# Value products summed by accumulating DMAs, and the ends of a scan and its corrections by VectorE

## The chip, the cores and the metric

The kernel runs on one core of a Trainium2 chip. The metric is device time in microseconds (us) of one execution; the median of several runs is compared. The core has TensorE (matmuls, into the PSUM memory), VectorE and ScalarE (elementwise work), GpSimd and SyncE, and sixteen DMA engines that the queues of SyncE, ScalarE and GpSimd feed. Each engine takes its instructions strictly in its written order, and an instruction that waits holds up all that stand behind it on its engine.

## What is computed

Two independent parts share the core, and their outputs are concatenated. Part A is a state space layer, part B a local, dilated attention:

```python
# A: x (1, 2048, 448), 448 complex states
Lam_bar = exp(dt * Lam);  B_bar = ((Lam_bar - 1) / Lam)[:, None] * Bmat
h[t] = Lam_bar * h[t-1] + B_bar @ x[t]
y = 2 * (h @ Cmat.T).real + x * Dskip
# B: 16 heads of 28, each token sees itself and 7 tokens at distances 2, 4 .. 14
attn = softmax(q . k[pos - 2*w] / sqrt(28) over w = 0..7, masked where pos - 2*w < 0)
o = sum over w of attn[w] * v[pos - 2*w];  out_b = o @ wo
```

## The kernel before

Part B holds 16 consecutive tokens in each of 128 partitions. Queries, keys and values come from TensorE, the logits from products on VectorE that TensorE sums, and the softmax weights `attn` are made for two halves of eight tokens. The value sums (`pv`, L437 and L440) are the longest work of VectorE: for each half two blocks of four tokens, so four blocks in all, in the order half 1 tokens 0 to 3, half 1 tokens 4 to 7, half 0 tokens 0 to 3, half 0 tokens 4 to 7. A block makes eight products `attn[w] * vd` of 128x1792 elements (L437), one for each w, and adds seven of them to the first (L440). The very last product and addition are cut into two halves. The tile `pvb` holds seven such arrays: three accumulators in turn and four products in turn. When a block is summed, `tail` transposes it by DMA on SyncE's queue into `oT` (L453), and TensorE multiplies it by `wo` (L462, `wo_ps`); the results are copied and stored.

Part A is a scan. With four tokens to a step, the level-1 sums of seven tiles m of 128 states (64 states, real and imaginary) are kept as `h[0]` to `h[3]`, each 128x512. A log-step scan (`scan`, L699 to L709) works on groups of sixteen tokens, for the tiles in three parts `MH` (0 to 3, 4 and 5, 6). Then:

- `ends` (L711) makes, for each m, the state at the end of every four tokens, `G[:, m]`. Seven matmuls go into one PSUM tile `gt` (L723): an identity matmul of 384 columns that brings in `h[3]`, five matmuls with powers of the transition, and an identity matmul of 128 columns that brings in the scan's result. ScalarE copies `gt` to `G` (L725).
- `correct` (L728) adds to `h[b][m]` (b from 0 to 2) what came in from earlier tokens, `mats[b + 1] @ G` (L733, PSUM tile `co`). Where VectorE does it, it adds `co` to `h` in place (L737) and `co` comes from the PSUM tag "pt" with two buffers. Where ScalarE does it (two of the 21), TensorE also adds `h` by an identity matmul (L732), ScalarE copies the sum back (L735), and the tag is "mm" with four buffers.
- `y` (L744) makes the output for 128 groups r and one of the four tokens b: four matmuls with the skip diagonal (L749) and seven with C (L753), a copy to `ya` (L756) and a store on SyncE's queue (L757).

The order of work in the last third is written out by hand. `vchain` chains VectorE's instructions, `chain` TensorE's. TensorE's list `line` holds the two corrections by ScalarE, the `wo` matmuls of the second block, sixteen `y` in the order b = 3, 0, 1, 2 (r from 0 to 3), the `wo` matmuls of the third block after (1, 3), and those of the fourth at the end. On VectorE, `each` is called for every operation of blocks three and four and, from the tenth on, puts one correction behind it. The matching `co` matmuls are spread over `line` by a count of estimated times:

```python
    for ins, dt in line:
        if n < len(extra) and t >= 1.55 * n:
            cx.chain(extra[n][0])
            t, n = t + extra[n][1], n + 1
```

GpSimd sets constants, gives small memsets that order matmuls (L139), and clears parts of `pbuf` and `G` in `alloc_scan`.

Of the kernel before, what the change touches and what calls it, by code (L numbers as in the profile page):

```python
# [12 lines left out]
ALU = mybir.AluOpType  # L13
AX = mybir.AxisListType
f32 = mybir.dt.float32
# [5 lines left out]
NCH = 128  # L21
# [15 lines left out]
PL = 64  # L37
NST = 7
PAD = 64
MH = ((0, 4), (4, 6), (6, 7))  # L40
# [3 lines left out]
KPOW = [1, 2, 3, 4, 8, 12] + [T << s_ for s_ in range(NST)]  # L44
NPW = len(KPOW)
BEGIN = [0, 20, 39]
WEAVE = [38, 55, 73, 85, 101, 112, 129, 140]


class Ctx:  # L50
# [41 lines left out]
    def vchain(self, ins):  # L92
        if self.vtail is not None:
            self.order(ins, self.vtail, "NoSync")
        self.vtail = ins

    def lanes(self, groups, weave=()):

# [62 lines left out]
class PartB:  # L161
# [94 lines left out]
    kdone, product = [0] * 8, None  # L256
# [166 lines left out]
    def pv(self, hf, at, jl0, jl1, last=False, between=(), each=lambda ins: None):  # L423
# [18 lines left out]
            yield between[w - 1](ins) if 0 < w <= len(between) else []  # L442
        self.outs.append(self.tail(hf, jl0, acc, last))

    def tail(self, hf, jl0, acc, last):
        nc, pool, cx = self.nc, self.pool, self.cx
        if self.oT is None:
            self.oT = pool.tile([KA, 2, 14, NCH], bf16, name="oT", tag="bX")
        oT, flat = self.oT[:, self.oi % 2], acc.rearrange("p j d h -> p (j d h)")
        self.oi += 1  # L450
        n = 7 if last else 14
        for c in range(0, 14, n):
            nc.sync.dma_start_transpose(oT[:, c:c + n], flat[:, c * KA:(c + n) * KA])  # L453

        def out(i):
            done = []
            for odd in range(2):
                n = D // 2 if last and i and odd else D
                for c, eng, q in ((0, "A", nc.sync), (n, "V", nc.scalar))[:D // n]:
                    ps = cx.ps([NCH, n], f32, "wo_ps", "lg" if n == D else "mm")  # L460
                    for k in range(KT):
                        done.append(nc.tensor.matmul(ps[:], lhsT=oT[:, 7 * i + 3 * odd + k, :], rhs=self.wo_p[:, odd, k, c:c + n],  # L462
                                                     start=(k == 0), stop=(k == KT - 1)).ins)
                    yb = cx.ya[:, 4 + 2 * i + odd] if last and n == D else pool.tile([NCH, n], bf16, name="yb", tag="yb", bufs=4)[:]
                    cx.ev(eng, yb, ps[:])
                    q.dma_start(self.out_b[:, hf * HJ + jl0 + 2 * i + odd, c:c + n], yb)
            return done

        return out if last else lambda: [out(i) for i in range(2)]


class PartA:
# [84 lines left out]
    def params(self, after):  # L557

        nc, pool, V, pt, kv = self.nc, self.pool, self.nc.vector, self.pt, self.kv
        ident = self.cx.ident  # L560

        def sm(name, shape):
            return pool.tile([NCH] + shape, f32, name=name)

        def wide(v):
# [27 lines left out]
        w, w4, ri = sm("w", [2, NM]), sm("w4", [2, 2, NM]), sm("ri", [2, NM])  # L593
# [13 lines left out]
        self.mats = {}  # L607

    def skip(self):
        nc, ident = self.nc, self.cx.ident  # L610
# [32 lines left out]
                  pool.tile([NCH, NM, 4 * NCH], bf16, name="h3", tag="pr", bufs=2)]  # L643

    def alloc_scan(self):
        pool = self.pool
        self.pbuf = [[pool.tile([NCH, m1 - m0, PAD + NCH], bf16, name=f"pbuf{m0}{i}", tag=f"pbuf{m0}{i}" if m0 else ("lgs", "e")[i]) for i in range(2)]
                     for m0, m1 in MH]
        for pb in self.pbuf:
            for t_ in pb:  # L650
                self.cx.order(self.nc.gpsimd.memset(t_[:, :, 0:PAD], 0.0).ins, self.cx.relay, "NoSync")
        self.G = pool.tile([NCH, NM, 2 + NF], bf16, name="G", tag="q0")
        self.cx.order(self.nc.gpsimd.memset(self.G[:, :, 0:1], 0.0).ins, self.cx.relay, "NoSync")

    def level1(self, mh):
        nc, cx = self.nc, self.cx
# [52 lines left out]
            nc.scalar.copy(dst[:, :, PAD:], ps[:])  # L709

    def ends(self, mh):  # L711
        nc, cx = self.nc, self.cx
        M, v = self.mats, self.h[3]
        hc = self.pbuf[mh][NST % 2]
        for m in range(*MH[mh]):
            vm = v[:, m, :]
            hp = hc[:, m - MH[mh][0], PAD - 1:PAD - 1 + NCH]
            ps = cx.ps([NCH, NF], f32, "gt", "mm")
            mm = [(cx.ident[:], vm[:, 0:3 * NCH], 0, 3), (M[4][:, m, :], vm[:, 0:2 * NCH], 1, 3),
                  (M[8][:, m, :], vm[:, 0:NCH], 2, 3), (M[4][:, m, :], hp, 0, 1), (M[8][:, m, :], hp, 1, 2),  # L720
                  (M[12][:, m, :], hp, 2, 3), (cx.ident[:], hc[:, m - MH[mh][0], PAD:PAD + NCH], 3, 4)]
            for i, (l_, r_, c0, c1) in enumerate(mm):
                nc.tensor.matmul(ps[:, c0 * NCH:c1 * NCH], lhsT=l_, rhs=r_, start=(i == 0), stop=(i == 6),  # L723
                                 skip_group_check=True)
# [231 lines left out]
```

## Time and profile before

| | |
|---|---|
| time, median of 3 runs | 140.66 us (140.31 to 140.9) |
| time of the profiled execution | 141.59 us |
| span of its instructions | 140.0 us |
| TensorE (PE) busy | 133.4 us, 95% |
| VectorE (DVE) busy | 125.0 us, 89% |
| ScalarE (ACT) busy | 86.3 us, 62% |
| GpSimd (POOL) busy | 10.2 us, 7% |
| mean TensorE clock granted | 0.995 of full speed |
| L437, products | 33, 34.5 us busy |
| L440, additions | 29, 30.5 us busy |
| L737, corrections by VectorE | 19, 13.0 us busy |

The profile is of one execution, and its span runs from the first to the last instruction; the remainder of its time lies around the span. The length given for a VectorE or TensorE instruction overlaps with the next one's, so a pace is read from start to start. A wait on a semaphore is named by the engine whose signal came last.

### The profile page before, as it was taken

To read this page: it belongs to the slowest core of one execution; us is meant where nothing else is said; L and a number is where in the kernel's file an instruction comes from. 1 tells how busy PE (TensorE), PEld (TensorE's weight loads), DVE (VectorE), ACT (ScalarE), POOL (GpSimd) and SP (SyncE) were. 2 spreads that over 40 slices of the span, in tenths; PEclk is the share of its full clock that TensorE was granted. 3 is DMA by queue.
4 is the path that set the end of the run, shared out by engine and by line. 5 is a ranking of instruction groups with operands and counts; after the bars stand their busy time and mean duration, and the time that the engine had idled before them with its cause. 6 is when DMAs were issued, how large, how long until landed. Compare 5 with 4: busy or idle time off the path is not lost.

```text
span 140.0 us, 3262 instructions
## 1 busy us (share of the span) xinstructions
PE 133.4 (95%) x1241; PEld 77.7 (56%) x1245; DVE 125.0 (89%) x159; ACT 86.3 (62%) x192; POOL 10.2 (7%) x104
## 2 busy tenths in 40 slices
PE   6999999999999999999999999999999999999970
PEld 2566544544676645455566655678555555555540
DVE  4589999989999999999999999999999999999010
ACT  2677678776785663695599868899633333344360
POOL 7301110001111001100120000000000000000000
PEclk9999999999999999999999999999999999999998
DMA  3999999999954979990024000532125521122842
GB/s 91 317 173 232 175 213 179 150 128 177 202 111 83 180 115 249 248 247 0 0 50 81 5 0 0 103 95 68 37 98 123 140 70 66 66 98 98 197 136 66
DMA packets 44798, 17.03 MB, mean 122 GB/s; under 512 B 37539, under 2 KB 44401, under 8 KB 44783
## 3 DMA queue, kind: packets, MB, share of 16 engines
q1 hardware_dynamic: 44309, 16.30, 56.4%
q10 hardware_dynamic: 474, 0.52, 1.1%
q8 instruction: 10, 0.16, 0.5%
q14 instruction: 5, 0.04, 0.1%
HBM read 3.91 MB, written 3.67 MB: 54 GB/s over the span
## 4 chain that ended last, share of the span: by engine, by line
PE 83%; ACT 10%; DVE 2%; issue 1%; POOL 0%; ACTq 0%; DVEq 0%
PE y_ps L753 15%; PE qk_ps L130 14%; PE v_ps L130 9%; PE l1h L130 8%; PE l L661 7%; PE wo_ps L462 6%; PE lg L346 6%; PE co L733 3%; PE gt L723 2%; PE warm L73 2%; PE y_ps L749 2%; PE l L706 2%; ACT pbuf L709 2%; ACT h L674 2%; ACT h L672 1%
## 5 line engine op out<-in xcount | busy, mean ns | idle before, releaser
L437 DVE TENSOR_TENSOR pvb<-attn,vd 128x1792 bf16<-128x1792 bf16 (+1 forms) x33 | 34.5, 1055 | 0.0
L440 DVE TENSOR_TENSOR pvb<-pvb 128x1792 bf16<-128x1792 bf16 (+1 forms) x29 | 30.5, 1051 | 0.2
L130 PE MATMUL qk_ps<-xbT,wqkv_nat 64*128 64x512 bf16 (+1 forms) x168 | 21.4, 351 | 0.1
L756 ACT CAST ya<-y_ps 128x448 bf16<-128x448 f32 x16 | 8.5, 532 | 18.9 <-PE y_ps L753 18.9
L335 DVE TENSOR_TENSOR pr<-q,kd 128x3072 bf16<-128x3072 bf16 x11 | 19.0, 1751 | 0.4 <-ACT q L156 0.4
L753 PE MATMUL y_ps<-Ccat,h 128*128 128x448 bf16 x84 | 19.0, 353 | 0.0
L130 PE MATMUL l1h<-xaT,Bcat 64*128 64x512 bf16 x112 | 15.7, 377 | 0.0
L462 PE MATMUL wo_ps<-wo_p,oT 128*128 128x448 bf16 (+1 forms) x68 | 14.3, 341 | 0.1
L130 PEld LDWEIGHTS <-wqkv_nat 64*128 64x128 bf16 x168 | 9.1, 94 | 8.5 <-POOL spot L139 1.9
L156 ACT CAST kd<-qk_ps 128x512 bf16<-128x512 f32 (+4 forms) x26 | 10.4, 426 | 5.0 <-PE qk_ps L130 4.4
L130 PE MATMUL v_ps<-wqkv_nat,xbT 64*128 64x448 bf16 x112 | 13.1, 360 | 0.0
L737 DVE TENSOR_TENSOR h<-co,h 128x512 bf16<-128x512 f32 x19 | 13.0, 686 | 0.0
L661 PE MATMUL l<-xaT,Bcat 128*128 128x512 bf16 x45 | 12.6, 379 | 0.1
L156 ACT CAST q<-qk_ps 128x512 bf16<-128x512 f32 (+2 forms) x23 | 9.9, 460 | 1.4 <-PE qk_ps L130 1.3
L753 PEld LDWEIGHTS <-h 128*128 128x128 bf16 x84 | 7.5, 98 | 5.6
L130 PEld LDWEIGHTS <-xbT 64*128 64x128 bf16 x112 | 7.4, 144 | 4.1 <-issue 1.4
L709 ACT CAST pbuf<-l 128x512 bf16<-128x512 f32 (+2 forms) x21 | 8.9, 426 | 1.0 <-PE l L706 0.8
L139 POOL MEMSET spot<- 1x1 f32 x59 | 5.2, 88 | 58.2 <-PE qk_ps L130 25.4
L156 ACT CAST vd<-v_ps 128x448 bf16<-128x448 f32 x16 | 7.6, 534 | 2.9 <-PE v_ps L130 2.8
L130 PEld LDWEIGHTS <-Bcat 64*128 64x128 bf16 x112 | 6.4, 94 | 5.2 <-issue 0.8
L462 PEld LDWEIGHTS <-oT 128*128 128x128 bf16 x68 | 6.4, 97 | 5.0 <-issue 0.2
L335 DVE TENSOR_TENSOR kd<-q,kd 128x3072 bf16<-128x3072 bf16 x5 | 8.8, 1753 | 0.5 <-ACT q L156 0.4
(135 smaller groups left out, 214.1 us busy)
## 6 DMA issues: line engine op xcount, KB each, us to landing
out_dram<-ya SPq DMA_DIRECT2D x19, 112.0 KB, 1.7
out_dram<-yb SPq DMA_DIRECT2D x12, 112.0 KB, 1.7
vd<-vd SPq DMA_DIRECT2D x1, 784.0 KB, 5.7
vd<-vd SPq DMA_DIRECT2D x1, 588.0 KB
xn<-in_B_x_dram SPq DMA_DIRECT2D x2, 224.0 KB, 2.7
wqkv_nat<-in_B_wqkv_dram ACTq DMA_DIRECT2D x2, 224.0 KB, 4.8
wqkv_nat<-in_B_wqkv_dram SPq DMA_DIRECT2D x2, 224.0 KB, 4.3
cn<-in_A_C_re_dram SPq DMA_DIRECT2D x4, 98.0 KB, 3.5
```

The source lines that it names most:

```text
L130: ins = mm(g["ps"], lhsT=l_, rhs=r_, start=first, stop=not (g["left"][0] or g["left"][1]), skip_group_check=True).ins
L156: return self.nc.scalar.copy(out, in_).ins
L335: self.queued(V.tensor_tensor(pr, q[0][:, qu].unsqueeze(2).to_broadcast([KA, KT - 1, 4, n]), self.shifted(self.kT[:, 2 * i + qu], s), op=A ...
L346: out.append(mm(lg[32 * t:32 * t + 32, n * qu:n * qu + n], lhsT=l_, rhs=r_, start=not (s or qu or c), stop=(s == 1 and c == KT - 1), skip_ ...
L437: each(V.tensor_tensor(t_[:, c0:c1], at[:, w, jl0 + c0:jl0 + c1, :].unsqueeze(2).to_broadcast([NCH, c1 - c0, DH, H]), self.vd[:, off + c0: ...
L440: ins = V.tensor_tensor(acc[:, c0:c1], acc[:, c0:c1], t_[:, c0:c1], op=ALU.add).ins
L462: done.append(nc.tensor.matmul(ps[:], lhsT=oT[:, 7 * i + 3 * odd + k, :], rhs=self.wo_p[:, odd, k, c:c + n], start=(k == 0), stop=(k == KT ...
L661: nc.tensor.matmul(ps[:], lhsT=self.Bcat[:, m, k, :], rhs=self.xT[:, b, k, :], start=(k == 0), stop=(b == 0 and k == KT - 1))
L709: nc.scalar.copy(dst[:, :, PAD:], ps[:])
L737: cx.vchain(nc.vector.tensor_tensor(h, ps[:], h, op=ALU.add).ins)
L753: out.append(nc.tensor.matmul(ps[:], lhsT=self.state(m, r, b), rhs=self.C[:, m, :], start=False, stop=(m == NM - 1), skip_group_check=True ...
L756: nc.scalar.copy(ya, ps[:])
```

## The change

- A new function `pv_paired` takes the place of `pv` for the second, third and fourth blocks. It makes the products of w = 0 to 5 in pairs; behind each pair GpSimd's queue issues a DMA that adds the pair's second product to its first, in SBUF (`accum_op=ALU.add`, 128x1792 elements): three DMAs to a block, nine in all. The products of w = 6 and 7 are added by VectorE, and then the three sums of the pairs: four additions to a block in place of seven. The product of w = 7 is written where the second product of the first pair was, and the accumulator is always `pvb[:, 0]`. In the fourth block only the last addition is cut in two; its products are whole.
- `ends` leaves out both identity matmuls. ScalarE copies the scan's result to the fourth token's places of `G`, once for each of the three parts, and for each m a new `join` on VectorE adds `gt` (now 384 columns) and `h[3]` into the other three. `JOINS` places one join behind operation 7 of blocks three and four, and six behind operation 9.
- All 21 corrections are VectorE's. From the tenth operation on, each is followed by two corrections in place of one, and the `co` matmuls stand at every 1.0 of the estimated time in place of 1.55.
- `gchain` keeps GpSimd's order: the memsets of `alloc_scan`, then the DMAs.

```diff
+JOINS = {7: 1, 9: 6}
...
+    def pv_paired(self, hf, at, jl0, each, last=False):
+        nc, V, n, b = self.nc, self.nc.vector, 4, self.pvb
...
+        for w in range(0, 6, 2):
+            t_, u_ = b[:, 1 + w], b[:, 2 + w]
+            product(w, t_)
+            product(w + 1, u_)
+            self.cx.gchain(nc.gpsimd.dma_start(t_.rearrange("p j d h -> p (j d h)"), u_.rearrange("p j d h -> p (j d h)"),
+                                               accum_op=ALU.add).ins)
+        acc, u_ = b[:, 0], b[:, 2]
+        product(6, acc)
+        product(7, u_)
+        add(acc, u_)
+        add(acc, b[:, 1])
+        add(acc, b[:, 3])
+        for c0, c1 in ((0, 2), (2, 4)) if last else ((0, 4),):
+            add(acc, b[:, 5], c0, c1)
+        self.outs.append(self.tail(hf, jl0, acc, last))
...
     def ends(self, mh):
-        hc = self.pbuf[mh][NST % 2]
-        for m in range(*MH[mh]):
+        hc, m0, m1 = self.pbuf[mh][NST % 2], *MH[mh]
+        Gv = self.G[:, :, 1:1 + NF].rearrange("p m (c a) -> p m a c", a=4)
+        nc.scalar.copy(Gv[:, m0:m1, 3], hc[:, :, PAD:PAD + NCH])
+        for m in range(m0, m1):
...
-            mm = [(cx.ident[:], vm[:, 0:3 * NCH], 0, 3), (M[4][:, m, :], vm[:, 0:2 * NCH], 1, 3),
-                  (M[8][:, m, :], vm[:, 0:NCH], 2, 3), (M[4][:, m, :], hp, 0, 1), (M[8][:, m, :], hp, 1, 2),
-                  (M[12][:, m, :], hp, 2, 3), (cx.ident[:], hc[:, m - MH[mh][0], PAD:PAD + NCH], 3, 4)]
+            mm = [(M[4][:, m, :], vm[:, 0:2 * NCH], 1, 3), (M[8][:, m, :], vm[:, 0:NCH], 2, 3), (M[4][:, m, :], hp, 0, 1),
+                  (M[8][:, m, :], hp, 1, 2), (M[12][:, m, :], hp, 2, 3)]
...
-            nc.scalar.copy(self.G[:, m, 1:1 + NF].rearrange("p (c a) -> p c a", a=4),
-                           ps[:].rearrange("p (a c) -> p c a", a=4))
+            self.joins.append((m, ps))
+
+    def join(self):
+        m, ps = self.joins.popleft()
+        self.cx.vchain(self.nc.vector.tensor_tensor(
+            self.G[:, m, 1:1 + NF].rearrange("p (c a) -> p a c", a=4)[:, 0:3], ps[:].rearrange("p (a c) -> p a c", a=3),
+            self.h[3][:, m, 0:3 * NCH].rearrange("p (a c) -> p a c", a=3), op=ALU.add).ins)
...
-    deque(b.pv(1, soft[1][1], 4, 8), 0)
     a.alloc_scan()
+    b.pv_paired(1, soft[1][1], 4, cx.vchain)
...
-    todo = [(b_, m) for b_ in range(3) for m in range(NM)][2:]
+    todo = [(b_, m) for b_ in range(3) for m in range(NM)]
...
-        if len(steps) >= 10 and todo:
-            extra.extend(a.correct(*todo.pop(0), "V"))
+        for n in range(JOINS.get(len(steps), 0)):
+            a.join()
+        if len(steps) >= 10:
+            for n in range(2):
+                if todo:
+                    extra.extend(a.correct(*todo.pop(0), "V"))
...
-    for m in range(2):
-        line += a.correct(0, m, "A")
     line += wo_line(wo[1]())
-    deque(b.pv(0, at0, 0, 4, each=each), 0)
-    deque(b.pv(0, at0, 4, 8, True, each=each), 0)
+    b.pv_paired(0, at0, 0, each)
+    b.pv_paired(0, at0, 4, each, True)
...
-        if n < len(extra) and t >= 1.55 * n:
+        if n < len(extra) and t >= n:
```

More of the change, by code (lines that the diff above doesn't have):

```diff
@@ L95, in vchain, with gchain @@
         self.vtail = ins
+    gtail = None
+    def gchain(self, ins):
+        if self.gtail is not None:
+            self.order(ins, self.gtail, "NoSync")
+        self.gtail = ins
     def lanes(self, groups, weave=()):
@@ L443, in pv, with product, add @@
         self.outs.append(self.tail(hf, jl0, acc, last))
+    def pv_paired(self, hf, at, jl0, each, last=False):
+        nc, V, n, b = self.nc, self.nc.vector, 4, self.pvb
+        def product(w, t_, c0=0, c1=n):
+            off = HALO + HJ * hf + jl0 - DIL * w
+            each(V.tensor_tensor(t_[:, c0:c1], at[:, w, jl0 + c0:jl0 + c1, :].unsqueeze(2).to_broadcast([NCH, c1 - c0, DH, H]),
+                                 self.vd[:, off + c0:off + c1], op=ALU.mult).ins)
+        def add(t_, u_, c0=0, c1=n):
+            each(V.tensor_tensor(t_[:, c0:c1], t_[:, c0:c1], u_[:, c0:c1], op=ALU.add).ins)
+        for w in range(0, 6, 2):
[13 more added lines that the diff above has]
+        self.outs.append(self.tail(hf, jl0, acc, last))
     def tail(self, hf, jl0, acc, last):
@@ L606, in params @@
                         ident[:, PL:NCH].unsqueeze(2).to_broadcast([NCH, PL, MP]), op=ALU.add)
-        self.mats = {}
+        self.mats, self.joins = {}, deque()
     def skip(self):
@@ L645, in alloc_scan @@
     def alloc_scan(self):
-        pool = self.pool
+        cx, pool = self.cx, self.pool
         self.pbuf = [[pool.tile([NCH, m1 - m0, PAD + NCH], bf16, name=f"pbuf{m0}{i}", tag=f"pbuf{m0}{i}" if m0 else ("lgs", "e")[i]) for i in range(2)]
                      for m0, m1 in MH]
+        cx.gchain(cx.relay)
         for pb in self.pbuf:
             for t_ in pb:
-                self.cx.order(self.nc.gpsimd.memset(t_[:, :, 0:PAD], 0.0).ins, self.cx.relay, "NoSync")
+                cx.gchain(self.nc.gpsimd.memset(t_[:, :, 0:PAD], 0.0).ins)
         self.G = pool.tile([NCH, NM, 2 + NF], bf16, name="G", tag="q0")
-        self.cx.order(self.nc.gpsimd.memset(self.G[:, :, 0:1], 0.0).ins, self.cx.relay, "NoSync")
+        cx.gchain(self.nc.gpsimd.memset(self.G[:, :, 0:1], 0.0).ins)
     def level1(self, mh):
@@ L713, in ends @@
         M, v = self.mats, self.h[3]
-        hc = self.pbuf[mh][NST % 2]
-        for m in range(*MH[mh]):
+        hc, m0, m1 = self.pbuf[mh][NST % 2], *MH[mh]
+        Gv = self.G[:, :, 1:1 + NF].rearrange("p m (c a) -> p m a c", a=4)
+        nc.scalar.copy(Gv[:, m0:m1, 3], hc[:, :, PAD:PAD + NCH])
+        for m in range(m0, m1):
             vm = v[:, m, :]
-            hp = hc[:, m - MH[mh][0], PAD - 1:PAD - 1 + NCH]
-            ps = cx.ps([NCH, NF], f32, "gt", "mm")
-            mm = [(cx.ident[:], vm[:, 0:3 * NCH], 0, 3), (M[4][:, m, :], vm[:, 0:2 * NCH], 1, 3),
-                  (M[8][:, m, :], vm[:, 0:NCH], 2, 3), (M[4][:, m, :], hp, 0, 1), (M[8][:, m, :], hp, 1, 2),
-                  (M[12][:, m, :], hp, 2, 3), (cx.ident[:], hc[:, m - MH[mh][0], PAD:PAD + NCH], 3, 4)]
+            hp = hc[:, m - m0, PAD - 1:PAD - 1 + NCH]
+            ps = cx.ps([NCH, 3 * NCH], f32, "gt", "mm")
+            mm = [(M[4][:, m, :], vm[:, 0:2 * NCH], 1, 3), (M[8][:, m, :], vm[:, 0:NCH], 2, 3), (M[4][:, m, :], hp, 0, 1),
+                  (M[8][:, m, :], hp, 1, 2), (M[12][:, m, :], hp, 2, 3)]
             for i, (l_, r_, c0, c1) in enumerate(mm):
-                nc.tensor.matmul(ps[:, c0 * NCH:c1 * NCH], lhsT=l_, rhs=r_, start=(i == 0), stop=(i == 6),
+                nc.tensor.matmul(ps[:, c0 * NCH:c1 * NCH], lhsT=l_, rhs=r_, start=(i == 0), stop=(i == 4),
                                  skip_group_check=True)
-            nc.scalar.copy(self.G[:, m, 1:1 + NF].rearrange("p (c a) -> p c a", a=4),
-                           ps[:].rearrange("p (a c) -> p c a", a=4))
+            self.joins.append((m, ps))
[4 more added lines that the diff above has]
+            self.h[3][:, m, 0:3 * NCH].rearrange("p (a c) -> p a c", a=3), op=ALU.add).ins)
     def correct(self, b, m, eng):
```

## The prediction

> **What bounds the kernel now.** I read the page's busy shares first, then the busy time by stretches, then VectorE's and TensorE's instructions in order of time from 70 us on, and last the DMA groups. The page:
>
> ```profile
> span 140.0 us, 3262 instructions
> ...
> PE 133.4 (95%) x1241; PEld 77.7 (56%) x1245; DVE 125.0 (89%) x159; ACT 86.3 (62%) x192; POOL 10.2 (7%) x104
> ...
> PE 83%; ACT 10%; DVE 2%; issue 1%; POOL 0%; ACTq 0%; DVEq 0%
> ```
>
> TensorE makes up 83% of the chain that ended last. But VectorE is close behind, and the stretches show how close (columns: length; busy us and count of PE, PEld, DVE, ACT, POOL; clock; DMA share; GB/s):
>
> ```profile
> 120.00:125.00 5.00, 5.00 (x31) 2.80 (x29) 5.00 (x8) 1.97 (x5) 0.00 (x0) 1.00 0.20 68
> 125.00:130.00 5.00, 5.00 (x37) 2.86 (x36) 4.44 (x7) 2.31 (x5) 0.00 (x0) 1.00 0.36 110
> ```
>
> Both engines are full up to 129.5 us, at full clock. VectorE in order of time (start, length, line, operation):
>
> ```profile
> 71.33 0.68 DVE L397 TENSOR_TENSOR attn<-e,rec 128x1024 bf16<-128x1024 bf16 x1
> 71.93 3.09 DVE L437 TENSOR_TENSOR pvb<-attn,vd 128x1792 bf16<-128x1792 bf16 x3
> ...
> 87.96 1.09 DVE L437 TENSOR_TENSOR pvb<-attn,vd 128x1792 bf16<-128x1792 bf16 x1
> 89.08 1.09 DVE L440 TENSOR_TENSOR pvb<-pvb 128x1792 bf16<-128x1792 bf16 x1
> 90.09 1.08 DVE L437 TENSOR_TENSOR pvb<-attn,vd 128x1792 bf16<-128x1792 bf16 x1
> ...
> 97.55 0.69 DVE L737 TENSOR_TENSOR h<-co,h 128x512 bf16<-128x512 f32 x1
> 98.16 1.08 DVE L440 TENSOR_TENSOR pvb<-pvb 128x1792 bf16<-128x1792 bf16 x1
> 99.20 0.69 DVE L737 TENSOR_TENSOR h<-co,h 128x512 bf16<-128x512 f32 x1
> ...
> 128.88 0.62 DVE L440 TENSOR_TENSOR pvb<-pvb 128x896 bf16<-128x896 bf16 x1
> ```
>
> From start to start a product or addition takes 1.005 us (89.08 to 90.09), 1.12 where an addition follows the very operation it needs (87.96 to 89.08), and a correction 0.605 (97.55 to 98.16). TensorE at the end of the corrections:
>
> ```profile
> 123.17 0.38 PE L733 MATMUL co<-G,mat 128*128 128x512 bf16 x1
> ...
> 124.71 0.38 PE L733 MATMUL co<-G,mat 128*128 128x512 bf16 x1
> 124.93 1.68 PE L462 MATMUL wo_ps<-wo_p,oT 128*128 128x448 bf16 x8
> 126.44 0.36 PE L749 MATMUL y_ps<-Dg,xaT 128*128 128x128 bf16 x4
> 126.64 1.49 PE L753 MATMUL y_ps<-Ccat,h 128*128 128x448 bf16 x7
> ```
>
> Corrections come every 1.54 us here, VectorE's pair of step and correction takes 1.605 us. A `co` matmul needs one of two PSUM buffers (tag "pt"), so it waits for the correction two before it. The last, at 124.71, waited for the one that VectorE started at 123.24 and ended at 123.92: 0.8 us to spare. TensorE is the bound, with VectorE 0.8 us behind.
>
> **The change part by part.** TensorE loses seven `gt` identity matmuls of 384 columns, seven of 128, and two `co` identities of 512: 4,608 columns, at 0.216 us for 512 (124.71 to 124.93) 1.94 us. ScalarE loses two `h` copies and exchanges seven `G` copies of 0.59 us for three; it is busy 62% and its end lies behind TensorE's, so this is worth nothing. VectorE loses nine additions (9 x 1.005 = 9.05 us) and gains seven joins and two corrections. No join is in the trace. The nearest row is the correction, the same addition from PSUM: 384/512 of 0.605 is 0.45, with a fixed part 0.47, which I take; bounds half a correction, 0.30, and a whole one, 0.605, that is -1.2 to +0.95 us over seven. So VectorE ends with 9.05 - 3.3 - 1.2 = 4.5 us less work.
>
> Both engines get lighter, but what counts is when a correction lets TensorE go on. Now every VectorE step brings two corrections: 1.005 + 2 x 0.605 = 2.215 us, 1.11 each. TensorE's written order places a `co` after each 1.0 us of its own line. So TensorE comes to wait for VectorE at the two buffers, with its y matmuls queued behind the waiting `co`. I therefore follow VectorE, from the first product of the second block, at 71.93 (nothing ahead of it changes):
>
> - second block: 12 x 1.005 + 4 dependent additions x 0.12 = 12.54, to 84.47;
> - third block: 7 products, a join, a product, an addition, 7.04 + 0.47 + 1.005 + 1.12, to 94.11; six joins, 2.82, to 96.93. The last `gt` group started at 96.56 before and now has six groups' identities (6 x 0.216 = 1.3 us) less ahead of it, so about 95.3; the last join is due at 96.46 and waits for nothing. The joins complete G, which all y matmuls need;
> - then steps of 2.215. The last `co` (number 20, from 0) waits for correction 18, in the tenth step: 96.93 + 9 x 2.215 + 1.005 + 0.69 = 118.56.
>
> Behind that `co` TensorE's order holds 56 y matmuls (8 x 1.32), seven groups of skip matmuls (7 x 0.20), 28 `wo_ps` of 448 columns (x 0.19) and eight of 224 (x 0.095): with the `co` 18.25 us, to 136.8. Before, it ran dry at 132.69 + 12 x 0.19 + 8 x 0.095 = 135.7. What follows (two copies, a store, the end) is unchanged. Sum: **+1.1 us**. The 1.94 us saved vanish in waits.
>
> This leaves out the DMAs. Each of nine adds 448 KB of SBUF into SBUF, on GpSimd's queue, behind its memsets (done at 71.4, with that softmax). VectorE waits for the first of each three at product 7, since that product overwrites the DMA's source. Everything later on VectorE, the joins too, is queued behind that product. In the second block the first DMA may take 5 x 1.005 - 0.08 = 4.95 us, the last 5.4; in the third block the first may take 5.4 (a join lies between), the others over 10. The fourth block has steps of 2.2 us and waits for none. The trace has no accumulating DMA. The nearest rows copy SBUF to SBUF (KB; us to landing):
>
> ```profile
> vd<-vd SPq DMA_DIRECT2D x1, 784.0 KB, 5.7
> wo_p<-wo_p SPq DMA_DIRECT2D x1, 224.0 KB, 2.8
> ```
>
> Interpolated, a plain copy of 448 KB takes 4.0 us. If reading the target counts as as many bytes again, 896 KB give 6.3. I take 5.0, between the two: at most 0.05 us of waiting. At 6.3 product 7 waits 1.35 us in the second block and 0.9 in the third, together +2.25; at 4.0 nothing. The Trainium skill ("DMA: Bandwidth & Descriptors", Anatomy of one DMA) fits a GpSimd DMA as 2.0 us plus bytes over 436 GB/s, so 3.05 us here, for copies; with it the sum stays +1.1. No row here shows it.
>
> Moves: SP's third oT transpose now stands ahead of the first ya store; its block ends at 96.93 + 2 x 2.215 + 1.0 = 102.4, before the first y is copied (some 103). The fourth block's two stand ahead of the store of the twelfth ya; VectorE ends at about 125.2, and only the sixteenth y needs that ya buffer, past 130. The last `wo_ps` come at 133.8; from VectorE's end to them it took 3.0 us before, 8.6 now. No cost, and 5 us of cover.
>
> The profiled execution took 141.59 us, span 140.0; the median shown is 140.66. The difference of +1.1 carries over: 141.8.
>
> **The rivals.**
>
> *Late DMAs.* Setup by GpSimd, a first use, or slow accumulation take the landing past 5.2 us. From there each us costs two, one in each of two blocks: 6 us gives +2.7 (143.4), 7.5 us gives +5.7 (146.4). For it: the upper row. Against: DMA is 0.08 busy from 80 to 90 us.
>
> *Descriptors held up.* A GpSimd DMA would start only when VectorE pauses, so at the wait of product 7: 5 us in each of two blocks, +10 beyond the sum, about 152. Against it in this trace:
>
> ```profile
> L139 POOL MEMSET spot<- 1x1 f32 x59 | 5.2, 88 | 58.2 <-PE qk_ps L130 25.4
> ```
>
> GpSimd wrote SBUF 39 times from 20 to 60 us in 88 to 89 ns each, with VectorE 99% busy. The Trainium skill ("SBUF — State Buffer", Summary: rules for kernel authors) says to move a GpSimd DMA off that queue rather than hide it under VectorE, whose 2x/4x modes starve its descriptors. By that rule it would be 152; the memsets speak against it.
>
> *TensorE stays the bound: faster.* If VectorE's chain finishes G 3 us earlier, at 94 rather than 96.93, or its pair of corrections takes under 2.0 us, the waits at the two buffers vanish and the 1.94 us come through: 138.7. For it: VectorE has 4.5 us less work in all. Against: most of that lies after the last correction, where nothing waits for it, and each duration of the chain is a row.
>
> **How the numbers follow.** My forecast has 0.59, late DMAs 0.25, held-up descriptors 0.04, TensorE as the bound 0.12. Forecast's own range: joins at 0.30 and no dependence costs give -0.7, joins at 0.605 and 0.2 us of DMA wait +2.3; so 140.0 to 143.0. Half a per cent is 0.7 us, about what can be told from no change. Of the forecast 0.14 falls within it, the rest above; of the last rival 0.10 is faster by more, 0.02 within. So faster 0.10, same 0.16, slower 0.74. The range leaves out some 0.10 below and 0.08 above: 140.4 to 146.0.
>
> **What would show it.** Right: additions only at the chained steps, nine GpSimd DMAs landing in 4 to 5 us, G complete at about 97, `co` spaced 2.2 us in pairs, with TensorE idle up to 2 us ahead of the third and 0.2 at every second, VectorE's sums done near 125, the last `wo_ps` from 133.8. Wrong: TensorE without gaps from 97 on (the last rival), or VectorE idle ahead of the eighth product (the DMAs).

## The result, and the profile after

| | before | after |
|---|---|---|
| time, median | 140.63 us (140.31 to 140.9) | 146.95 us (146.35 to 147.97) |
| time and span of the profiled execution | 141.59 and 140.0 us | 146.35 and 144.2 us |
| additions of products by VectorE (L440 before; L448 and L463 after) | 29 | 20 |
| start of the last `wo_ps` group | 132.52 us | 137.56 us |

The change made the kernel slower: the ratio is 1.0458, with a 95% interval of 1.0385 to 1.0531. The forecast was 141.8 us with a range of 140.4 to 146.0, so the direction was right, and the size lay outside the range.

The page of after, first the span and the busy shares, then the shares by engine of the chain that ended last, then the group of the nine DMAs (448 KB each, median us from issue to landing):

```profile
span 144.2 us, 3250 instructions
PE 133.1 (92%) x1225; PEld 76.8 (53%) x1229; DVE 123.2 (85%) x158; ACT 83.6 (58%) x186; POOL 17.9 (12%) x113
DVE 47%; PE 36%; issue 11%; DMA 3%; ACT 1%; POOL 0%; DVEq 0%; POOLq 0%
pvb<-pvb POOLq DMA_DIRECT2D x9, 448.0 KB, 4.9
```

TensorE made up 83% of that chain before. Now VectorE makes up 47% of it, although VectorE has less to do than before (123.2 us busy, 125.0 before). Behind the start-up, TensorE waits for VectorE in one stretch only, from 96 us on (1.1 us for joins and 2.9 us ahead of `co`). Why VectorE comes late there, its order of time shows (start, length, line; in brackets the wait ahead of the instruction, and for what):

```profile
71.87 8.10 DVE L459 TENSOR_TENSOR pvb<-attn,vd 128x1792 bf16<-128x1792 bf16 x8
80.00 3.35 DVE L463 TENSOR_TENSOR pvb<-pvb 128x1792 bf16<-128x1792 bf16 x3
84.81 1.09 DVE L463 TENSOR_TENSOR pvb<-pvb 128x1792 bf16<-128x1792 bf16 x1 [1.47 <-DMA pvb<-pvb]
85.82 7.09 DVE L459 TENSOR_TENSOR pvb<-attn,vd 128x1792 bf16<-128x1792 bf16 x7
92.84 1.02 DVE L768 TENSOR_TENSOR G<-gt,h 128x384 bf16<-128x384 f32 x1
...
95.81 5.37 DVE L768 TENSOR_TENSOR G<-gt,h 128x384 bf16<-128x384 f32 x6
100.99 1.10 DVE L463 TENSOR_TENSOR pvb<-pvb 128x1792 bf16<-128x1792 bf16 x1
```

Two things are longer than forecast. VectorE waits 1.47 us for a DMA ahead of the second block's last addition. And the six joins from 95.81 to 100.99 take 5.18 us, 0.863 us each from start to start, where 0.47 was forecast. G is complete at 100.99, not at 96.93. On TensorE:

```profile
98.12 1.89 PE L498 MATMUL wo_ps<-wo_p,oT 128*128 128x448 bf16 x8
102.74 0.38 PE L777 MATMUL co<-G,mat 128*128 128x512 bf16 x1 [2.73 <-DVE h L781]
...
104.94 0.38 PE L777 MATMUL co<-G,mat 128*128 128x512 bf16 x1 [0.17 <-DVE h L781]
...
107.14 0.38 PE L777 MATMUL co<-G,mat 128*128 128x512 bf16 x1
...
122.52 0.38 PE L777 MATMUL co<-G,mat 128*128 128x512 bf16 x1
...
137.56 3.22 PE L498 MATMUL wo_ps<-wo_p,oT 128*128 128x448 bf16 x20
```

TensorE sits idle for 2.73 us ahead of the third `co`, as the forecast said it would (it gave up to 2 us), then 0.17 us at a later one, and goes on in steps of 2.2 us for two corrections (104.94 to 107.14). Before, it had no idle time there.

The DMAs of the second block, issued 2.0 us apart, land one after the other (the DMA group of three windows, one DMA in each, in the order of issue):

```profile
pvb<-pvb POOLq DMA_DIRECT2D x1, 448.0 KB, 4.4
pvb<-pvb POOLq DMA_DIRECT2D x1, 448.0 KB, 5.4
pvb<-pvb POOLq DMA_DIRECT2D x1, 448.0 KB, 6.5
```

Each takes longer than the one before, and the last is the one that VectorE waits for at 84.81. Waiting in line for the DMA engines is a part of this only. While the third DMA moved its data, a load of instructions (queue q8, 16 KB) held one of the sixteen engines for 0.94 us from 81.14. Below are its line (window 79.5 to 82 us) and the busy share of the DMA engines in 40 slices from 82 to 86 us:

```profile
q8 instruction: 1, 0.02, 2.4%
DMA  9999999972200100101001000000000000000000
```

The engines are full up to 83 us; then single packets follow up to 84.4. In the trace's packet records each of these DMAs ends with sixteen packets of 4 bytes, taken here as one from each engine: for the third DMA fifteen came by 83.28 us and the last at 84.42, 1.1 us later. The third block's DMAs, also 2.0 us apart, had no such load among their packets:

```profile
pvb<-pvb POOLq DMA_DIRECT2D x1, 448.0 KB, 4.3
pvb<-pvb POOLq DMA_DIRECT2D x1, 448.0 KB, 4.9
pvb<-pvb POOLq DMA_DIRECT2D x1, 448.0 KB, 5.8
```

### The profile page after: what moved, and what is told of

The parts are those of the page before. It is cut to its first block, busy times and chain, and to the rows that moved or that the text cites. A ratio compares the mean times of both kernels' runs of the same rounds, so it can differ in the third digit from the quotient of the medians.

```text
span 144.2 us, 3250 instructions
## 1 busy us (share of the span) xinstructions
PE 133.1 (92%) x1225; PEld 76.8 (53%) x1229; DVE 123.2 (85%) x158; ACT 83.6 (58%) x186; POOL 17.9 (12%) x113
## 4 chain that ended last, share of the span: by engine, by line
DVE 47%; PE 36%; issue 11%; DMA 3%; ACT 1%; POOL 0%; DVEq 0%; POOLq 0%
PE qk_ps L138 14%; DVE pvb L459 10%; DVE h L781 8%; PE y_ps L797 7%; DVE pvb L445 5%; DVE pvb L448 4%; PE lg L354 4%; PE wo_ps L498 4%; DVE mat L666 3%; DMA pvb<-pvb 3%; DVE G L768 3%; PE v_ps L138 3%; DVE pr L343 2%; PE warm L74 2%; DVE pvb L463 2%
## 5 line engine op out<-in xcount | busy, mean ns | idle before, releaser
L459 DVE TENSOR_TENSOR pvb<-attn,vd 128x1792 bf16<-128x1792 bf16 x24 | 25.0, 1083 | 0.0
L463 DVE TENSOR_TENSOR pvb<-pvb 128x1792 bf16<-128x1792 bf16 (+1 forms) x13 | 13.1, 1016 | 1.7 <-DMA pvb<-pvb 1.5
L781 DVE TENSOR_TENSOR h<-co,h 128x512 bf16<-128x512 f32 x21 | 13.5, 681 | 0.0
L469 POOL DMA_DIRECT2D pvb<-pvb x9 | 7.8, 864 | 40.2 <-DVE pvb L459 40.2
L164 ACT CAST yb<-wo_ps 128x448 bf16<-128x448 f32 (+1 forms) x13 | 6.9, 533 | 7.9 <-PE wo_ps L498 7.9
L777 PE MATMUL co<-G,mat 128*128 128x512 bf16 x20 | 7.6, 378 | 3.4 <-DVE h L781 2.9
```

What stands on the lines that cost most here:

```text
L164: return self.nc.scalar.copy(out, in_).ins
L459: each(V.tensor_tensor(t_[:, c0:c1], at[:, w, jl0 + c0:jl0 + c1, :].unsqueeze(2).to_broadcast([NCH, c1 - c0, DH, H]), self.vd[:, off + c0: ...
L463: each(V.tensor_tensor(t_[:, c0:c1], t_[:, c0:c1], u_[:, c0:c1], op=ALU.add).ins)
L469: self.cx.gchain(nc.gpsimd.dma_start(t_.rearrange("p j d h -> p (j d h)"), u_.rearrange("p j d h -> p (j d h)"), accum_op=ALU.add).ins)
L781: cx.vchain(nc.vector.tensor_tensor(h, ps[:], h, op=ALU.add).ins)
```

## The experiments

The theory after the first reading: the mechanism of the forecast is right (VectorE completes G late, and the pairs of corrections then pace TensorE), but the joins and the DMAs were priced too low. The rivals: TensorE is held by the two buffers of `co` or by the spacing in its written order, whatever the joins cost; or the DMAs as such cost more than the additions that they replace. In the DMA groups each time runs from issue to landing. The time measured for a run is the median, with the lowest and highest; its ratio is to the kernel before as timed beside it (medians of 140.63 to 141.03 us). The edits are shown against the change and are abridged.

**1. The order in which a join walks its elements.** The join writes three of every four elements of G. In the change it goes token by token, so neighbouring writes lie 8 bytes apart; here it goes group by group, three neighbours at a time.

```
-  rearrange("p (c a) -> p a c", a=4)[:, 0:3], ps[:].rearrange("p (a c) -> p a c", a=3), (h likewise)
+  rearrange("p (c a) -> p c a", a=4)[:, :, 0:3], ps[:].rearrange("p (a c) -> p c a", a=3), (h likewise)
```

> The seven joins run over their elements in the order token group, then token, so that three neighbouring elements of G are written in turn, and gt and h[3] are read with a stride instead. Theory A (the joins are slow because their output steps by 8 bytes): a join falls from 0.86 us from start to start to about 0.47, G is complete 2.7 us earlier, at about 98.3, and the time falls by 2.7 us. Rival B (a join is slow for what it reads or waits for, PSUM or TensorE): it stays at 0.86 or grows, and the time does not fall.

Measured: 143.77 us (143.53 to 144.2), ratio 1.0216 (1.0187 to 1.0245). The groups of tile G, in after and then here (min/median/max in ns, first and last start):

```profile
L768 DVE TENSOR_TENSOR G<-gt,h x7: 1014/1053/1082, 92.8 to 100.1; 128x384 bf16<-128x384 f32 x7
L754 ACT COPY G<-pbuf x3: 496/779/1353, 81.1 to 95.6; 128x512 bf16<-128x512 bf16 x1, 128x256 bf16<-128x256 bf16 x1, 128x128 bf16<-128x128 bf16 x1
```

```profile
L768 DVE TENSOR_TENSOR G<-gt,h x7: 550/552/555, 93.2 to 98.2; 128x384 bf16<-128x384 f32 x7
...
95.84 2.88 DVE L768 TENSOR_TENSOR G<-gt,h 128x384 bf16<-128x384 f32 x6
98.63 1.08 DVE L463 TENSOR_TENSOR pvb<-pvb 128x1792 bf16<-128x1792 bf16 x1
```

The same join takes half as long: six from 95.84 to 98.63, 0.465 us each, almost to the hundredth the 0.47 of the forecast. Only the order changed, and the reads went from plain order to steps, so the writes at a step of 8 bytes are what doubled it. G is complete 2.36 us earlier, and the profiled span is 2.4 us shorter (141.8). ScalarE's copies of the fourth tokens into G have the same step, and they are slow too: 1.353 us for 512 elements, where the old copy of 512 into G in plain order, from PSUM, took 0.59 (no run changes this order alone). That comes back in experiment 10.

**2. The ends as before.** TensorE's identities and ScalarE's copy sum the four tokens again, and VectorE has no joins; the DMAs and the corrections stay as in the change.

```
-  nc.scalar.copy(Gv[:, m0:m1, 3], ...); five matmuls; self.joins.append((m, ps))
+  mm = [(ident, vm[:, 0:3 * NCH], 0, 3), ..., (ident, hc, 3, 4)]; nc.scalar.copy(G[:, m], ps)
-  for n in range(JOINS.get(len(steps), 0)): a.join()
```

> The ends of four tokens are made as in the kernel before (identity matmuls on TensorE, ScalarE copies gt to G); there are no joins. DMAs and corrections stay as changed. Theory A: G is complete when ScalarE has copied it, at about 98, and the first correction starts at about 97.6 instead of 102.0, 4.4 us earlier; TensorE has 1.5 us more matmuls, but ahead of that point; the time falls by about 4 us, to about 1.5 to 2 us over the kernel before. Rival C (DMA traffic is what costs): the time falls by less than 2.5 us.

Measured: 142.44 us (142.27 to 142.8), ratio 1.0121 (1.0096 to 1.0146). The last `co` comes at 118.67 and the last `wo_ps` group at 133.71, 3.85 us before that of after. So the ends by VectorE are the larger part of the loss. The DMA wait is here too (1.47 us), but it costs nothing: VectorE afterwards sits idle for 1.36 us ahead of its first correction, at 97.58, until TensorE has made its `co`. What is left against before is the pace of the corrections, which experiment 8 shows.

**3. Two DMAs in the second block.** The middle one of its three is replaced by an addition on VectorE.

```
+  if hf and w == 2:
+      add(t_, u_)
+      continue
   self.cx.gchain(nc.gpsimd.dma_start(t_..., u_..., accum_op=ALU.add).ins)
```

> The kernel after with the second of the second block's three accumulating DMAs replaced by an addition on VectorE. Theory (the third DMA landed after 6.5 us because it queued behind two others on the same 16 DMA engines): with 4 us or more between two issues the third lands after 4.4 to 4.9 us, VectorE's 1.47 us of waiting ahead of the last addition go, the addition costs 1.1 us, and the joins end 0.3 us earlier: about 100.6, the time 146.0 us where the clock stays full. Rival (a third DMA is slow by where it stands, for instance by GpSimd's descriptors or by what else VectorE and ScalarE do at that time): it lands again after 6 us or more.

Measured: 145.89 us (145.85 to 146.43), ratio 1.0343 (1.0293 to 1.0392). The two remaining DMAs of the second block:

```profile
pvb<-pvb POOLq DMA_DIRECT2D x1, 448.0 KB, 4.3
pvb<-pvb POOLq DMA_DIRECT2D x1, 448.0 KB, 4.2
```

VectorE around them:

```profile
81.15 4.47 DVE L463 TENSOR_TENSOR pvb<-pvb 128x1792 bf16<-128x1792 bf16 x4
85.54 7.10 DVE L459 TENSOR_TENSOR pvb<-attn,vd 128x1792 bf16<-128x1792 bf16 x7
```

The DMA that landed after 6.5 us now lands after 4.2, and no wait is left ahead of the four additions. Its place in the block and its size are the same; the rival of its place is out. Two things are gone: the DMA just ahead of it, and the instruction load among its packets, which here ran from 79.49 to 80.45, before this DMA's first packet at 80.86. So this run doesn't part the two. With none ahead of it, a DMA of this kind took 4.2 to 4.4 us in the second and third blocks; in the fourth block of after, issued 4.4 us apart and beside stores of `ya`, the three took 4.5, 4.5 and 5.0. Waiting in line alone shows in the third block of after, with 4.3, 4.9 and 5.8 us. The load shows in every run with three DMAs in the second block: a load of 0.89 to 1.23 us, and one engine that closes the third DMA 0.9 to 1.3 us behind the other fifteen. The addition takes back 1.1 of the 1.47 us.

**4. The waiting addition moved behind other work.** The first two products of the third block go ahead of the second block's last addition.

```
+  product(0, b[:, 1], 0, n, *lead)      # the third block's w = 0 and 1
+  product(1, b[:, 2], 0, n, *lead)
   add(acc, b[:, 5], c0, c1)
```

> The first two products of the third block stand ahead of the last addition of the second block, which waits for the third DMA; no work is added or removed. Theory A (that wait of 1.47 us lies on VectorE's chain, which sets the end up to the last co): the wait goes, G is complete 1.5 us earlier, the time falls by 1.5 us. The first DMA of the third block is then issued up to 2 us sooner against its own limit and should still land in time. Rival C (the DMAs slow the kernel by their traffic, and the wait only stands where a later one would): the wait comes back elsewhere and the time stays within 0.5 us.

Measured: 149.37 us (148.36 to 149.79), ratio 1.062 (1.0583 to 1.0657), slower than after by 2.4 us. The wait of 1.47 us went, and a larger one came:

```profile
93.84 1.09 DVE L459 TENSOR_TENSOR pvb<-attn,vd 128x1792 bf16<-128x1792 bf16 x1 [3.46 <-DMA oT<-pvb]
```

The third block's seventh product overwrites the accumulator that the second block's transpose still reads. That transpose could only start after the later addition, and it shares the DMA engines with the accumulating DMAs of the third block. In after, its time was hidden. This is a miss of the experiment's design, and it shows how close the next wait stood. The windows of this run, 1 us each, show something else (columns: length; busy us and count of PE, PEld, DVE, ACT, POOL; clock; DMA share; GB/s):

```profile
97.00:98.00 1.00, 0.25 (x5) 0.17 (x3) 1.00 (x2) 0.17 (x1) 0.00 (x0) 1.00 0.74 249
98.00:99.00 1.00, 0.13 (x1) 0.13 (x1) 1.00 (x2) 0.00 (x0) 0.00 (x0) 0.67 0.00 0
99.00:100.00 1.00, 0.91 (x7) 0.71 (x7) 1.00 (x2) 0.00 (x0) 0.00 (x0) 0.50 0.00 0
100.00:101.00 1.00, 1.00 (x7) 0.66 (x6) 1.00 (x2) 0.00 (x0) 0.00 (x0) 0.50 0.07 16
```

TensorE's granted clock falls to 0.50 while TensorE has little to do, and stays there when work is back. Experiment 9 is about that.

**5. No DMAs.** All nine additions go back to VectorE, everything else as in the change.

```
-  self.cx.gchain(nc.gpsimd.dma_start(t_..., u_..., accum_op=ALU.add).ins)
+  self.cx.vchain(V.tensor_tensor(t_, t_, u_, op=ALU.add).ins)
```

> The nine additions that GpSimd's DMAs make are made by VectorE at the same places; everything else is as changed. Theory A (up to the last co the end follows VectorE's chain): three more additions of 1.1 us in the second block in place of the wait of 1.47 us, and three more ahead of the joins in the third: G complete about 5.2 us later, and about 5 us more time, 152. Rival C (the DMAs cost more by their traffic and queueing than they take off VectorE): the time falls or stays.

Measured: 154.44 us (153.8 to 154.85), ratio 1.0948 (1.0899 to 1.0997). G is complete at 106.24 instead of 100.99 and the last `co` comes at 130.79. So in this order of work the DMAs are worth 7.5 us, even with their wait: the rival that they cost more than the additions is out. Here too the clock fell to 0.50 behind an idle time of TensorE of 4.22 us, so not all of the 7.5 us is VectorE's work.

**6. More buffers, or wider spacing, alone.** First, every second `co` from the fifth on takes a buffer of another PSUM tag, so four buffers serve instead of two.

```
-  "mm" if eng == "A" else "pt"
+  "lg" if 7 * b + m >= 4 and (7 * b + m) % 2 == 0 else "pt"
```

> From co number 4 on, every second co takes a PSUM buffer of the tag lg instead of pt, so that a co waits for the correction four before it instead of two. Theory A (TensorE is held at the two buffers by VectorE's pace): the last co starts with the end of correction 16 instead of 18, 2.2 us earlier, and the time falls by about 2 us, with the gaps of 0.2 us ahead of every second co gone. Rival D (the gaps of TensorE are its own, and the late end comes from work behind the last co): no change.

Measured: 145.51 us (144.44 to 146.48), ratio 1.0334 (1.0263 to 1.0405); the last `wo_ps` group starts at 135.96. Second, a `co` after every 1.25 us of TensorE's line instead of every 1.0 us:

```
-  if n < len(extra) and t >= n:
+  if n < len(extra) and t >= 1.25 * n:
```

> One number: co matmuls at every 1.25 of the estimated time in place of 1.0, slower than VectorE's 1.11 us for each; joins and DMA waits stay. Theory A: TensorE no longer stands in front of a full pair of buffers, except once until the first corrections, and spends that time on y matmuls; it has some 33 us of work after the joins are complete at 101, so its end comes about 2.3 us sooner and the time falls to about 144.5. Rival D (TensorE is held by the late G alone, the spacing has no part): within 0.5 us of the changed kernel.

Measured: 145.44 us (143.97 to 145.64), ratio 1.0286 (1.0236 to 1.0336); the last `wo_ps` group starts at 136.50, although the last `co` has moved back to 126.20. In the traces each gives back 1.1 to 1.6 us of the 5.04 that the group came later. The second trace had a mean clock of 0.988, though; its two executions at full clock took 143.97 and 144.18 us, some 2.3 us less than the two of after at full clock, which is what was expected. The wait of 2.35 to 2.73 us ahead of the third `co` stays in both, since that wait is for G. So the buffers and the spacing are a part of the loss, and not its root.

**7. All terms as the forecast had them.** The joins by groups, the late addition, and for the third block an accumulator of its own, so that the wait of experiment 4 can't come.

```
+  acc = self.pool.tile([NCH, 4, DH, H], bf16, name="own", tag="pr", bufs=2)[:] if own else b[:, 0]
```

> Joins in the order token group, then token; two products of the third block ahead of the second block's last addition; and the third block sums into a tile of its own, so that it need not wait for the second block's transpose. The two terms that the sum had too small are gone, spacing and number of corrections are as changed. Theory A: G complete at about 97.0, the last co at about 118.6, the time of the forecast: 1.1 us over the kernel before, 141.8. Rival D (there is a further cost in the change that the sum lacks): 143 or more.

Measured: 143.19 us (142.71 to 143.62), ratio 1.0155 (1.0117 to 1.0193). G is complete at 98.02, the last `co` comes at 119.53 and the last `wo_ps` group at 134.58; the forecast had 96.93, 118.56 and 133.8. So about 1 us of the forecast's chain is still missing, and it is in place before G is complete:

```profile
92.63 0.56 DVE L772 TENSOR_TENSOR G<-gt,h 128x384 bf16<-128x384 f32 x1 [0.96 <-ACT yb L164]
```

The first join waits. The copy that the profile names started at 91.99 and is no input of the join; the join's own `gt` group had its last matmul at 92.53, and that fits. TensorE is late there because, earlier, it waited for ScalarE:

```profile
83.25 0.22 PE L737 MATMUL l<-h,ident 128*128 128x128 bf16 x1 [0.58 <-ACT h L715]
```

ScalarE's copy of `h` stood behind the strided copy of the fourth tokens, 1.34 us long, that had started at 81.44.

**8. The same with the spacing that VectorE's pace allows**, 1.25 us; and the ends as before with that spacing.

> The kernel with both terms mended (joins in the other order, no wait for the third DMA, an accumulator of its own) and co matmuls at every 1.25. Theory A: nothing holds TensorE after 98 us, and of the 1.94 us of matmuls that the change takes off it some 1.4 to 1.9 come through: 138.8 to 139.3, faster than the kernel before. Rival D: no faster than 140.7, since the removed matmuls lay beside VectorE's work anyway.

Measured: 140.78 us (140.66 to 141.28), ratio 0.999 (0.9966 to 1.0015): equal to before, and not the 1.5 to 2 us faster that was expected. TensorE waits only 0.44 us from 96 us on.

> The kernel after with the ends as before (ends summed by TensorE's identities and copied by ScalarE, no joins), and a correction's matmul placed after every 1.25 us of TensorE's line instead of 1.0. Theory (VectorE holds TensorE at the two buffers only where the matmuls stand closer than VectorE's 1.11 us a correction): with 1.25 TensorE waits for no correction, the last correction's matmul moves back but the last group on wo_ps starts at about 132.1, against 133.71 with the spacing of 1.0; 140.3 us (139.9 to 141.0). Rival (G is complete too late in any case): unchanged against the same kernel with 1.0, 142.4 us.

Measured: 141.04 us (140.67 to 142.07), ratio 1.0007 (0.9974 to 1.004). The last `wo_ps` group starts at 131.88 (132.1 expected), the median is just above the expected range. So with the corrections spaced for VectorE, the DMAs cost nothing; they bring nothing either, since TensorE is the bound again.

**9. TensorE's idle time filled.** Ten matmuls on zeros ahead of the third `co` of after.

```
+  fps = cx.ps([NCH, NF], f32, "fill", "mm")
+  fill = [nc.tensor.matmul(fps[:], lhsT=cx.wz[:, 0:NCH], rhs=cx.wz[:], start=True, stop=True).ins for _ in range(10)]
```

> The kernel after with ten matmuls of 512 columns on zeros (10 x 0.216 = 2.16 us, into a PSUM buffer that nothing reads) in TensorE's order just ahead of the third correction's matmul, where TensorE sat idle for 2.73 us. Nothing waits for them. Theory (the granted clock falls because TensorE sits idle, so it is the idle time and not the wait that costs the extra 1.2 to 1.4 us of span in about half of the executions of after): the mean granted clock is 0.995 or more in every execution, every span lies at 144.1 to 144.4 us, and the time is 146.4 us (146.2 to 146.6). Rival (the clock falls for another reason): some executions again show a mean clock of 0.986 to 0.988 and a span of 145.3 to 145.8 us, and the median is about 147.

Measured: 146.53 us (146.13 to 147.2), ratio 1.04 (1.0364 to 1.0435); mean clocks of 1.0, 0.997, 0.996, 1.0, 1.0 and 0.995. TensorE in the place of the gap:

```profile
99.77 2.32 PE L958 MATMUL fill<-wz 128*128 128x512 bf16 x10
102.68 0.38 PE L777 MATMUL co<-G,mat 128*128 128x512 bf16 x1 [0.59 <-DVE h L781]
```

Of the four executions of after, two had a mean clock of 0.988 and 0.986 and spans of 145.8 and 145.3 us, against 144.2 and 144.3. Of the four kernels with this gap of more than 2.3 us (after, and those of experiments 3 and 6), 9 of 18 executions had a mean clock of 0.988 or less; with the gap filled none of six had. The time moved as expected, but three of the six spans are 144.5 to 145.1 us at clocks of 0.995 to 0.997, above the 144.4 expected. So the theory is supported and not settled.

**10. The strided copy out of the way.** Experiment 8's first kernel, with ScalarE's first copy of fourth tokens behind the last copy of the scan.

```
   four = nc.scalar.copy(Gv[:, m0:m1, 3], hc[:, :, PAD:PAD + NCH]).ins
+  if mh == 0:
+      cx.order(four, self.lastscan, "NoSync")
```

> The run of all four edits (joins in the order of groups, the third block's first products ahead of the second's last addition, an accumulator of its own, spacing 1.25; 140.78 us) with ScalarE's first copy of the fourth tokens put behind the last copy of the scan. Theory (this copy, 1.34 us at 81.44, holds up the copies of h that TensorE waits for): TensorE's 0.58 us of waiting at 83.25 go, the first group on gt is 0.5 us earlier, the first join waits 0.4 instead of 0.96 us, and the time is 140.3 us (140.1 to 140.5). Rival (the first join waits for something else, or TensorE is full behind it anyhow): 140.8 us.

Measured: 140.22 us (139.96 to 140.72), ratio 0.9945 (0.9917 to 0.9973). TensorE's 0.58 us are gone, and the first join waits 0.37 us:

```profile
91.73 0.56 DVE L774 TENSOR_TENSOR G<-gt,h 128x384 bf16<-128x384 f32 x1 [0.37 <-ACT yb L164]
...
94.34 2.88 DVE L774 TENSOR_TENSOR G<-gt,h 128x384 bf16<-128x384 f32 x6
97.13 1.08 DVE L463 TENSOR_TENSOR own<-own,pvb 128x1792 bf16<-128x1792 bf16 x1
```

G is complete at 97.13, 0.2 us from the forecast's 96.93, and the last `wo_ps` group starts at 131.40. This version is faster than both kernels, against before by half a per cent, little more than can be told from no change.

## Why the forecast failed in size

**What held.** VectorE's chain, not TensorE's work, sets the end, and the 1.94 us of matmuls saved vanish in waits. From G complete to the last `co` the forecast had 21.63 us, the trace has 122.52 - 100.99 = 21.53; from there to the last `wo_ps` group 15.24, the trace 15.04. The steps of 2.2 us, the pairs and (read from start to start) the 0.2 us of waiting are there. The whole miss lies ahead of G complete, in two terms of the sum, and in the last step that carried the difference over to the median. A third term, ScalarE's three copies into G, was taken as nothing: it cost nothing here, where VectorE came later still, but 1 us of G's time showed once the other two were mended (experiments 7 and 10). One misreading had no effect: GpSimd's memsets were done at 72.9 us, not 71.4.

**The joins (taken 0.47, bounds 0.30 to 0.605).** They took 0.81 for the first and 0.863 for the others: 0.81 + 5.18 - 7 x 0.47 = +2.70 us. The step that failed is the choice of row. The correction reads PSUM and adds just as the join does, but writes in plain order; the join's own line in the diff shows a write with a step of four elements, and the bounds did not allow for that. Experiment 1, which changes only this, measured 0.465.

**The DMAs (taken 5.0, at most 0.05 us of waiting).** A single one took 4.2 to 4.4 us, better than taken, and the first of each block was in time for product 7, where the forecast and its rival looked for the wait. But the forecast gave all three one landing time, as if each had the sixteen DMA engines to itself. Two issued 2.0 us apart overlap: 5.4, then 6.5 us, against the limit of 5.4 that the forecast had worked out for the third (5.1 from the issue, which came 0.3 us after the product that it waits for). Ahead of the last addition that cost 1.47 us, and the second block ended 85.82 - 84.47 = 1.35 us late. Had the sixteenth engine closed the third DMA with the others, the wait would have been some 0.3 us (1.47 less 1.14, an estimate); so most of it goes back to the instruction load, for which the forecast had no term. That the load is what held this engine is read from the order of the packets; no run moves the load alone. With 2.70 the 1.35 us make 4.05 of the 4.06 us by which G was late.

**From the profiled execution to the median (taken as unchanged).** On the profiled executions the forecast was 141.59 + 1.1 = 142.69, and 146.35 came: +3.66, the 4.06 us above less 0.4 of small gains behind G. The other 1.5 us of the miss are no work of the chain. The profiled execution of before lay 0.93 us above its median, so that the difference to be carried over was too small by that. Most of it stands at its end, which the forecast took as unchanged: from the start of the last `wo_ps` group to the end of the span it took 7.5 us, against 6.6 in after and 6.2 to 6.7 in the experiments. Of all the traces it alone has an instruction load there (0.95 us from 135.86), and SyncE's issue of its last store took 1.21 us, in after 0.38. In the 3.66 us this hardly shows, since the time outside the span was 0.56 us longer in after (2.15 against 1.59). And the median of after lies 0.60 above its profiled execution, because two of the four executions were longer, at mean clocks of 0.988 and 0.986 (experiment 9).

**The rivals.** *Late DMAs* came in part, but through the third DMA instead of the first, once instead of twice, and at 1.47 us. *Descriptors held up* did not come: GpSimd's part of the three DMAs took 0.84 to 0.99 us each, while VectorE ran eight products without a pause (71.87 to 80.00):

```profile
74.28 0.99 POOL L469 DMA_DIRECT2D pvb<-pvb  x1 [1.43 <-DVE pvb L459]
76.27 0.86 POOL L469 DMA_DIRECT2D pvb<-pvb  x1 [1.00 <-DVE pvb L459]
78.26 0.84 POOL L469 DMA_DIRECT2D pvb<-pvb  x1 [1.13 <-DVE pvb L459]
```

The rule of the Trainium skill ("SBUF — State Buffer", Summary: rules for kernel authors) does not show in this kernel: the first of these landed in 4.4 us under a busy VectorE. *TensorE stays the bound* needs G at 94; it came at 101. Experiment 10 reached it in another way, by a spacing that VectorE can follow, and then 0.7 of the 1.94 us came through against the median of before. Where the remainder goes stays open; up to 96 us TensorE also waits for the scan's copies, and the matmuls saved there are no time saved.

## What to carry to other kernels

An operand's step in memory belongs in its price: look for a row with the same step, on the same engine, before you take one with the same operation and size. Where several DMAs are issued closer together than the DMA engines need for one, price the last of them and not the typical one, and look for the wait at whoever needs the last. A transfer over all sixteen engines ends with its slowest engine, so see which other queue has packets at that time. A time that is carried over from one profiled execution is worth a second look when it stands well above or below the median, here by 0.93 us, nearly as much as the whole forecast difference; its end, set beside another trace's, tells where.

## What the hardware showed that was not expected

- A write with a step of 8 bytes (every fourth 16-bit element) doubled VectorE's addition from PSUM, 0.863 against 0.465 us for 384 elements. ScalarE's copy with the same step took 1.353 us for 512 against 0.59 in plain order (that one from PSUM, so the step isn't shown apart). The Trainium skill ("SBUF — State Buffer", Specifications (TRN2)) says that two accesses to each 16-byte line are enough for full bandwidth; a step of 8 bytes has two, and it was not free here.
- An accumulating DMA of 448 KB from SBUF to SBUF took 4.2 to 4.4 us alone, and as the second and third of a train issued every 2.0 us 4.9 and 5.8 us, or 5.4 and 6.5 where a load of instructions shared one engine with the third. The Trainium skill's fit ("DMA: Bandwidth & Descriptors", Anatomy of one DMA) gives an estimate of 3.05 us; the measurement is 1.2 us or more above it.
- A load of 16 KB of instructions (queue q8) took 0.89 to 1.23 us of one of the sixteen DMA engines in the runs with three DMAs in the second block, and one engine closed the accumulating DMA that it fell into 0.9 to 1.3 us behind the others (experiment 3).
- The granted clock fell to 0.50 behind stretches in which TensorE was sparse but never idle for more than 1.63 us at a time (experiment 4, where all four executions show it, with mean clocks of 0.962 to 0.988); in after it fell in two of four executions. The Trainium skill ("TensorE: Matmul & The Clock Gate", Part 1: The HAM clock gate) tells of a half clock after an idle window of about 3.4 us that runs freely; the 0.50 and the change from one execution to the next agree, the length of the idle time does not.
